# Five instead of three weight pieces converted beside the MoE, and the second layer from step 42

## The chip, the cores and the metric

The kernel runs on one NeuronCore of a Trainium2 chip. The metric is the device time of one execution in microseconds. A core has five engines that run side by side and wait for each other by semaphores: TensorE (PE in the profile; its weight loads are shown apart as PEld), VectorE (DVE), ScalarE (ACT), GpSimd (POOL) and SyncE (SP), which here only issues transfers. Each engine takes its instructions strictly in the order in which the program lists them.

## The reference

An attention of 4 batches, 8 heads, 576 tokens and 64 columns per head, with rotary embedding, feeds a gated MLP ("MoE" below):

```
scores = scale * matmul(rotate(q), rotate(k).T)
x      = softmax(scores) @ v              # back to (batch, 576, 512)
h      = maximum(x @ w_in, 0)             # w_in: 512 x 1024, first layer
gate   = sigmoid(conv3(h))                # three taps along the tokens
out    = (h * gate) @ w_out               # w_out: 1024 x 512, second layer
```

The weights come to the chip as 64-bit floats, seen as pairs of 32-bit integers. They are converted to fp32 on the chip.

## The kernel before

**Steps.** The attention is cut into 16 head pairs (p) of 5 row blocks (s), 80 steps in all. In a step PE forms one block of scores (L258), DVE takes the negated row maximum (`negm`, L266), ACT the exponential (`st`, L270), PE transposes the result one step later (`tp`, L318), ACT copies it out (`pt`, L197), and in the next five steps the product with v follows (L395), is copied to `xn` and normalised (`norm`, L413). POOL applies the rotary embedding to q and k (L188, L191; 18 instructions for a head pair), DVE transposes them into `qT` and `kT` (L231, L234).

**Two stages.** In steps 0 to 25 ("narrow") only attention and the conversion of weights run. From step 26 (`WIDE`) the MoE's work is woven in: `UNITS` says in which steps a first-layer unit (M1, L450 or L460) is formed, `HALVES` in which steps half a tile of the second layer (M2, L572: 48 matmuls into two PSUM tiles, then `oh` copied by ACT, L586, and added by DVE, L587). One step uses one pair of PSUM tiles `pm` (`m_pair`); whatever the step forms in `pm`, units, halves or products with v, shares that pair. The products with v of a head pair are formed in the steps that five divides (30, 35, 40, 45, 50).

**The order** is written out by hand: `at(n, rank, fn)` puts a piece of work into step n, and within a step the ranks sort it. All engines keep that order.

**The weights** are 16 pieces of 128x512: eight of `w_in` (0 to 7), then eight of `w_out` (8 to 15). A piece is one load of 512 KB, an ACT instruction (L598) and four DVE instructions: clamp (L601), shift (L607), low (L612), third (L617). A `w_out` piece is then split into a high part (ACT, L672) and a low part (POOL, four instructions, L669); of a `w_in` piece this is done later by `split_win` (L436, L439), in the steps of `SPLIT`. Pieces 0 to 12 are converted in steps 0 to 25, spread evenly by `COST`; `LATEW` lists the steps and ranks of the other three, between 25 and 35. M2 needs all eight `w_out` pieces, M1 the first four `w_in` low parts from step 46 and the other four from step 51.

**Memory.** The early pieces use the pool `ws`, whose memory goes to the MoE's tiles at step 26; the late pieces use a pool `wl` of their own, 12 KB of each partition, whose end at step 38 makes room for the tile `gb` (gated activations). `winh`, 16 KB of each partition, holds the high parts of `w_in`; nothing stands in it before step 39.

**The tail** after step 79 runs the rest of M1 and M2 alone.

Of the kernel before, what the change touches and what calls it, by code (L numbers as in the profile page):

```python
# [7 lines left out]
F32 = mybir.dt.float32  # L8
F32R = mybir.dt.float32r
# [11 lines left out]
def attention_moe_kernel(ctx, tc, q, k, v, w_in, conv_w, w_out, tab, tabx, out):  # L21
# [31 lines left out]

    winh = keep.tile([128, NK, DFF], F32R, name="winh")
    winp = ctx.enter_context(tc.tile_pool(name="winp", bufs=2 * NK + 1))
# [376 lines left out]
    def split_win(i):  # L432
        c, kk = divmod(i, NK)
        hi = winh[:, kk, 512 * c:512 * c + 512]
        lo = lows[kk, c] = winp.tile([128, 512], F32R, tag="w", name="wlo")
        nc.scalar.activation(out=hi, in_=raws[kk, c], func=AF.Copy)  # L436
        for o in range(0, 512, 128):
            w = slice(o, o + 128)
            nc.gpsimd.tensor_tensor(out=lo[:, w], in0=raws[kk, c][:, w], in1=hi[:, w].bitcast(F32), op=ALU.subtract)  # L439

    def emit_M1(blk, f, last=False):
# [6 lines left out]
        if plain(blk):  # L448
            for kk in range(NK):
                nc.tensor.matmul(  # L450
                    out=ps[:, 0:XW], lhsT=raws[kk, half][:, gs], rhs=xraw[kk, j], start=(kk == 0), stop=(kk == NK - 1)
                )
        else:
            n = 3 * NK
            i = 0
            for kk in range(NK):
                xs = xslot[b, kk, j]
                hi, lo = winh[:, kk, fs], lows[kk, half][:, gs]
# [132 lines left out]

    def to_f32(pool, bufs, w64, n):
        w32 = w64.bitcast(I32).rearrange("p (n t) -> p n t", t=2)
        h, l = w32[:, :, 1], w32[:, :, 0]
        t = pool.tile([128, n], I32, tag="wt", name="wt", bufs=bufs)[0:w64.shape[0]]

# [36 lines left out]
    def load_w(i):  # L633
        src, _, _, kk, c = WPIECES[i]
        pool, bufs = wpool(i)
        t = pool.tile([128, 512], I64, tag="w64", name="w64", bufs=bufs + 1)
        nc.sync.dma_start(out=t, in_=src[kk * 128:kk * 128 + 128, c:c + 512])
        stage[i] = t

    def conv_w_piece(i):  # L640
# [3 lines left out]
        def first():  # L644
            box["s"] = to_f32(*wpool(i), stage.pop(i), 512)
            box["s"][0]()
# [4 lines left out]
        def last():  # L651
            pool, bufs = wpool(i)
            if dl is None:
                box["w"] = raws[kk, c // 512] = winp.tile([128, 512], F32, tag="w", name="wr")
            else:
                box["w"] = pool.tile([128, 512], F32, tag="wf", name="wf", bufs=bufs)
            box["s"][4](box["w"])
            if i + 4 < WEARLY:
                load_w(i + 4)
            elif WEARLY <= i < len(WPIECES) - 2:  # L660
                load_w(i + 2)
            if dl is None:
# [39 lines left out]

    lctx = ExitStack()
    ws = wctx.enter_context(tc.tile_pool(name="ws", bufs=2))
    wl = lctx.enter_context(tc.tile_pool(name="wl", bufs=1, side="right"))

    def wpool(i):
        return (ws, 3) if i < WEARLY else (wl, 1)

    wcv = [conv_w_piece(i) for i in range(len(WPIECES))]  # L710
    WEARLY = len(wcv) - 3
    COST = (0, 0.5, 0.6, 0.85, 0.85)
    wsteps = [(0, wcv[0][0])]
    for i in range(WEARLY):
# [9 lines left out]
    LATEW = (  # L724
# [3 lines left out]
    )  # L728
    plan = {}
    onpe = (0, 0.2, 0.5, 1, 2, 2.4, 3, 4, 10)  # L730
    engines = {nc.tensor.engine, nc.vector.engine, nc.scalar.engine, nc.gpsimd.engine, nc.sync.engine}

    def at(n, rank, fn):
        plan.setdefault(n, []).append((rank, len(plan.get(n, [])), fn))

    def emit():
        with tc.manual_schedule(engines=engines):
# [83 lines left out]
            while any(plan.values()):  # L821
                n += 1
                late["n"] = n
                if n == WIDE:
# [87 lines left out]
```

## Time and profile before

| | |
|---|---|
| median of 3 runs | 475.98 us (475.81 to 476.61) |
| the profiled execution: its own time | 476.06 us |
| its span, first to last instruction | 474.3 us |
| PE busy / DVE busy / ACT busy / POOL busy | 457.1 / 352.3 / 327.9 / 293.0 us |
| granted TensorE clock | 1.00 throughout (the 2.4 GHz level) |

The engine shares are means over stages with different limits, so they are read stage by stage below. A step's start is taken as the start of its score matmuls (L258, eight instructions): step 36 begins at 152.0 us, 37 at 157.8, 40 at 172.7, 41 at 179.1, 42 at 184.9, 45 at 200.5 and 46 at 206.9 us.

### The profile page before, as it was taken

The numbers are of one execution on the slowest core, as the hardware profiler recorded it, in microseconds if no ns is written. First come the engines' busy times: TensorE is split into PE (matmuls) and PEld (weight loads), VectorE is DVE, ScalarE is ACT, GpSimd is POOL, SyncE is SP. The second block draws the span as 40 slices with busy tenths as digits, with TensorE's granted clock in tenths as the row PEclk, the third lists the DMA queues.
The fourth block names the chain that finished last, engine by engine and source line by source line (L and its number), as shares of the span: only waits on it lengthen the run. The fifth ranks groups of instructions, "written<-read, shape, count | busy, mean of one in ns | idle before, by whom it ended". The sixth has DMA issues, their size and how long they took to land.

```text
span 474.3 us, 12267 instructions
## 1 busy us (share of the span) xinstructions
PE 457.1 (96%) x4563; PEld 357.8 (75%) x4563; DVE 352.3 (74%) x641; ACT 327.9 (69%) x942; POOL 293.0 (62%) x478
## 2 busy tenths in 40 slices
PE   8789998989999999999999999999999999999997
PEld 7355655656666877778797978888797878899886
DVE  4799999986999886678677777866765747468921
ACT  2779889886897886879596877868686854244510
POOL 3859596998689694997939392938430332144610
PEclk9999999999999999999999999999999999999999
DMA  9798778362570716016161625135010000100011
GB/s 242 189 218 208 190 170 184 93 167 69 121 143 11 138 37 118 21 48 127 37 139 37 127 49 114 51 82 104 27 49 29 24 25 2 46 23 23 0 68 44
DMA packets 103183, 42.63 MB, mean 90 GB/s; under 512 B 94524, under 2 KB 97876, under 8 KB 103124
## 3 DMA queue, kind: packets, MB, share of 16 engines
q1 hardware_dynamic: 102672, 41.50, 37.3%
q8 instruction: 36, 0.59, 0.5%
q10 hardware_dynamic: 452, 0.35, 0.2%
q14 instruction: 23, 0.19, 0.1%
HBM read 37.04 MB, written 4.79 MB: 88 GB/s over the span
## 4 chain that ended last, share of the span: by engine, by line
PE 70%; DVE 13%; ACT 6%; POOL 3%; DMA 3%; issue 2%; SPq 1%; DVEq 0%; POOLq 0%; ACTq 0%
PE sp L258 11%; PE mt L552 11%; PE pm L395 10%; PE pm L572 10%; PE pm L460 9%; PE mt L460 7%; PE pm L450 5%; PE tp L318 5%; DVE negm L266 4%; ACT st L270 3%; POOL rk L188 2%; ACT pt L197 1%; DMA rq<-q 1%; DVE wt L601 1%; DVE wr L617 1%
## 5 line engine op out<-in xcount | busy, mean ns | idle before, releaser
L266 DVE TENSOR_REDUCE negm<-sp 128x1 f32<-128x576 f32 x144 | 102.5, 748 | 29.5 <-PE sp L258 22.2
L270 ACT ACTIVATE st<-sp,negm 128x576 f32<-128x576 f32 x128 | 93.8, 740 | 26.6 <-DVE negm L266 22.4
L258 PE MATMUL sp<-kT,qT 64*128 64x288 f32 (+4 forms) x556 | 94.5, 450 | 0.9 <-ACT kT L197 0.7
L197 ACT ACTIVATE pt<-tp 128x512 f32<-128x512 f32 (+3 forms) x176 | 84.5, 533 | 5.0 <-PE tp L318 4.3
L481 DVE SCALAR_TENSOR_TENSOR c<-rr,cw,c 128x288 f32<-128x288 f32 x128 | 79.3, 619 | 4.2
L499 POOL TENSOR_TENSOR gm<-c,gm 128x288 fp32r<-128x288 f32 (+4 forms) x72 | 45.7, 639 | 48.4 <-ACT gm L498 48.2
L188 POOL TENSOR_TENSOR rq<-rq,tabt 128x192 f32<-128x192 f32 x90 | 60.8, 709 | 18.1 <-DMA rq<-q 16.4
L188 POOL TENSOR_TENSOR rk<-rk,tabt 128x192 f32<-128x192 f32 x90 | 58.9, 687 | 8.0 <-DVE negm L266 4.3
L258 PEld LDWEIGHTS sp<-kT,qT 64*128 64x128 f32 (+1 forms) x556 | 44.8, 174 | 22.8 <-issue 9.8
L318 PEld LDWEIGHTS tp<-idf,st 64*128 64x128 f32 x1024 | 41.4, 139 | 21.9 <-ACT st L270 10.6
L318 PE MATMUL tp<-idf,st 64*128 64x64 f32 x1024 | 47.2, 227 | 6.5 <-ACT st L270 5.3
L395 PE MATMUL pm<-pt,vm 128*64 128x290 f32 x368 | 49.8, 411 | 0.4 <-ACT pt L197 0.4
L572 PE MATMUL pm<-wouth,gm 64*128 64x256 f32 x512 | 49.6, 284 | 0.0
L490 DVE SCALAR_TENSOR_TENSOR c<-c,rr 128x288 f32<-128x288 f32 x64 | 38.0, 614 | 9.5 <-ACT c L487 9.5
L479 DVE TENSOR_SCALAR c<-rr,cw 128x288 f32<-128x288 f32 x56 | 24.9, 444 | 23.2 <-ACT rr L471 22.9
L572 PEld LDWEIGHTS pm<-wouth,gm 64*128 64x128 f32 x512 | 41.5, 186 | 0.0
L420 POOL TENSOR_TENSOR xT<-xn,xT 128x290 fp32r<-128x290 f32 x18 | 16.0, 890 | 40.2 <-ACT xT L416 40.2
L395 PEld LDWEIGHTS pm<-pt,vm 128*64 128x64 f32 x368 | 25.5, 137 | 17.9 <-ACT pt L197 1.1
L460 PE MATMUL pm<-xT,winh 128*128 128x290 f32 x176 | 37.0, 302 | 0.0
L572 PE MATMUL pm<-woutl,gm 64*128 64x256 f32 x256 | 36.9, 278 | 0.0
L487 ACT ACTIVATE c<-c 128x288 f32<-128x288 f32 x64 | 28.5, 445 | 10.8 <-DVE c L481 10.8
L450 PE MATMUL pm<-xr,wr 128*128 128x290 f32 x128 | 34.5, 417 | 0.0
(127 smaller groups left out, 970.4 us busy)
## 6 DMA issues: line engine op xcount, KB each, us to landing
rq<-q SPq DMA_DIRECT2D x60, 144.0 KB
rk<-k SPq DMA_DIRECT2D x60, 144.0 KB
w<-moe_w_in SPq DMA_DIRECT2D x8, 512.0 KB
vm<-v SPq DMA_DIRECT2D x32, 128.0 KB
w<-moe_w_out SPq DMA_DIRECT2D x8, 512.0 KB
rb<-rd SPq DMA_DIRECT2D x16, 144.0 KB
out<-oh SPq DMA_DIRECT2D x18, 128.0 KB
rb<-rd SPq DMA_DIRECT2D x16, 128.0 KB
```

Of the source, the lines that this page charges most:

```text
L188: nc.gpsimd.tensor_tensor(out=y, in0=y, in1=tabt[:, a:a + 3], op=ALU.mult)
L197: nc.scalar.activation(out=out, in_=in_, func=AF.Copy, scale=1.0 if sc is None else sc)
L258: nc.tensor.matmul(out=out, lhsT=qt[64 * h:64 * h + 64, c], rhs=kt[64 * h:64 * h + 64, a:a + n], start=True, stop=True)
L266: reds.setdefault((p, s), []).append(lambda: nc.vector.tensor_reduce(out=nm, in_=sc, axis=AX.XY if len(sc.shape) == 3 else AX.X, op=ALU.ma ...
L270: lambda: nc.scalar.activation(out=dst, in_=sc, func=AF.Exp, bias=nm, scale=1.0, accum_out=sm)
L318: nc.tensor.transpose(ps[r][:, 64 * k:64 * k + 64], x[i], idf[i, i])
L395: nc.tensor.matmul(out=xp[64 * h:64 * h + 64, :], lhsT=vmain[p][:, h, i, :] if i < 4 else vrem[p % 2][:, h, :], rhs=pt[:, 2 * i + h if i < ...
L450: nc.tensor.matmul(out=ps[:, 0:XW], lhsT=raws[kk, half][:, gs], rhs=xraw[kk, j], start=(kk == 0), stop=(kk == NK - 1))
L460: nc.tensor.matmul(out=ps[:, 0:XW], lhsT=w, rhs=x_at(xs, e), start=(i == 0), stop=(i == n - 1))
L481: nc.vector.scalar_tensor_tensor(out=c, in0=r[:, j + e:j + e + HS], scalar=cw[:, 8 * e + f:8 * e + f + 1], in1=c, op0=ALU.mult, op1=ALU.add,)
L552: nc.tensor.matmul(out=ops[tt][:, 0:width], lhsT=g_tile(tt, f, e), rhs=w[:, f, cols], start=(f == 0 and i == 0), stop=(f == NF - 1 and i = ...
L572: nc.tensor.matmul(out=ps[r][:, 0:256], lhsT=g_tile(tt, f, e)[rows], rhs=w[rows, f, cols], start=(f == 0 and i == 0), stop=(f == NF - 1 an ...
```

## The change

`WEARLY` falls from 13 to 11: pieces 11 and 12 take the three late places of before, and pieces 14 and 15 get two new ones, in steps 35 to 38 and 38 to 41. The late pieces no longer have a pool of their own. A pool `highp` of two buffers of 8 KB takes the memory of `winh`: each late piece has one buffer for its load, its scratch and its result ("room"), and later the two buffers hold the high parts of the two halves of `w_in` (`wh`). The loads have steps of their own (`LOADW`). `gb` is there from step 26. M2 now starts at step 42: the halves of steps 37 and 39 move on, and two steps get a half that had none, 45 and 50. `SPLIT` moves by one or two steps.

```diff
-    winh = keep.tile([128, NK, DFF], F32R, name="winh")
+    highp = ctx.enter_context(tc.tile_pool(name="highp", bufs=2))
+    winh = {}
...
-        hi = winh[:, kk, 512 * c:512 * c + 512]
+        if c not in winh:
+            winh[c] = highp.tile([128, 4 * 512], F32R, tag="h", name="wh").rearrange("p (k n) -> p k n", k=NK)
+        hi = winh[c][:, kk, :]
...
-        t = pool.tile([128, 512], I64, tag="w64", name="w64", bufs=bufs + 1)
+        if i < WEARLY:
+            t = ws.tile([128, 512], I64, tag="w64", name="w64", bufs=4)
+        else:
+            room[i] = highp.tile([128, 4 * 512], F32, tag="h", name="room")
+            t = room[i].bitcast(I64)[:, 0:512]
...
-    WEARLY = len(wcv) - 3
+    WEARLY = len(wcv) - 5
...
-    HALVES = [37, 39, 42, 44, 47, 49, 52, 54, 57, 59, 62, 64, 67, 68, 72, 73, 76, 78]
+    HALVES = [42, 44, 45, 47, 49, 50, 52, 54, 57, 59, 62, 64, 67, 68, 72, 73, 76, 78]
...
-    SPLIT = (39, 40, 42, 43, 44, 45, 47, 48)
+    SPLIT = (40, 42, 44, 45, 46, 47, 49, 50)
...
+        ((35, 5.5), (36, 2.6), (36, 2.6), (37, 2.6), (37, 2.6)),
+        ((38, 5.5), (39, 2.6), (39, 2.6), (40, 2.6), (40, 2.6)),
     )
+    LOADW = (22, 23, 29, 33, 36)
```

The first place is DVE in steps 37 to 39, before. `c` rows are the MoE's convolution and gate, `xn` the normalising, `oh` the sum of a half of M2.

```order
L266 TENSOR_REDUCE negm<-sp 128x1 x2
L479 TENSOR_SCALAR c<-rr_1623,cw 128x288
L481 SCALAR_TENSOR_TENSOR c<-rr_1623,cw,c 128x288 x2
L413 TENSOR_TENSOR xn<-xn,rb 128x290 x2
L587 TENSOR_TENSOR oh<-oh,pm 128x256
L266 TENSOR_REDUCE negm<-sp 128x1 x2
L490 SCALAR_TENSOR_TENSOR c<-c,rr_1622 128x288
L490 SCALAR_TENSOR_TENSOR c<-c,rr_1623 128x288
L479 TENSOR_SCALAR c<-rr_1624,cw 128x288
L481 SCALAR_TENSOR_TENSOR c<-rr_1624,cw,c 128x288 x2
L266 TENSOR_REDUCE negm<-sp 128x1
```

The same place in the change. The `room` rows are the conversion of piece 14.

```order
L605 TENSOR_SCALAR room<-room 128x512
L611 TENSOR_SCALAR room<-room 128x512
L267 TENSOR_REDUCE negm<-sp 128x1 x2
L482 TENSOR_SCALAR c<-rr_1593,cw 128x288
L484 SCALAR_TENSOR_TENSOR c<-rr_1593,cw,c 128x288 x2
L414 TENSOR_TENSOR xn<-xn,rb 128x290
L616 SCALAR_TENSOR_TENSOR room<-room 128x512
L621 SCALAR_TENSOR_TENSOR room<-room 128x512
L414 TENSOR_TENSOR xn<-xn,rb 128x290
L267 TENSOR_REDUCE negm<-sp 128x1 x2
L493 SCALAR_TENSOR_TENSOR c<-c,rr_1592 128x288
```

Between the row maxima of steps 36 and 38 four conversion rows have come in and one `oh` row has gone; piece 15 follows in the same way in steps 39 and 40.

The second place is PE in step 37, before: scores, transposes, and the first of the 17 rows (48 matmuls) of a half of M2.

```order
L258 MATMUL sp<-kT,qT 128x288 x4
L318 MATMUL tp<-idf,st 128x64 x16
L355 MATMUL pm<-idf,st 128x64 x2
L572 MATMUL pm<-wouth,gm 128x256 x2
L572 MATMUL pm<-woutl,gm 128x256 x2
L572 MATMUL pm<-wouth,gm 128x256 x4
```

The same place in the change, steps 37 to 39; `pm<-xr` are the two units of M1 of step 38.

```order
L259 MATMUL sp<-kT,qT 128x288 x4
L319 MATMUL tp<-idf,st 128x64 x16
L356 MATMUL pm<-idf,st 128x64 x2
L259 MATMUL sp<-kT,qT 128x288 x4
L319 MATMUL tp<-idf,st 128x64 x16
L356 MATMUL pm<-idf,st 128x64 x2
L453 MATMUL pm<-xr,wr 128x290 x8
L259 MATMUL sp<-kT,qT 64x288 x4
```

Step 37 now holds scores and transposes alone, and step 39 (the `sp` of 64 rows) likewise; the 48 matmuls of each have moved on.

The third place is PE at the end of step 45, before: the products with v, straight behind the transposes (`tp`). The numbers tell the PSUM tiles apart.

```order
L318 MATMUL tp_3125<-idf_82,str_0_88 128x64
L395 MATMUL pm_3160<-pt_100,vm_2649 64x290 x8
L395 MATMUL pm_3160<-pt_100,vr_0_86 64x290 x2
L395 MATMUL pm_3161<-pt_100,vm_2649 64x290 x8
L395 MATMUL pm_3161<-pt_100,vr_0_86 64x290 x2
```

The same place in the change: the last two rows of the half that has come there, and the products behind it.

```order
L575 MATMUL pm_3011<-wouth_81,gm_1605 128x256
L575 MATMUL pm_3012<-wouth_81,gm_1605 128x256
L396 MATMUL pm_3011<-pt_102,vm_2517 64x290 x8
L396 MATMUL pm_3011<-pt_102,vr_0_88 64x290 x2
L396 MATMUL pm_3012<-pt_102,vm_2517 64x290 x8
L396 MATMUL pm_3012<-pt_102,vr_0_88 64x290 x2
```

The products write the two tiles that the half has just filled, so they wait until ACT and DVE have read them; before, no step held both. Step 50 is alike.

## Rows read from the trace of the kernel before

**Rows 1.** The page, part 1: busy time, share of the span, instructions of each engine.
```profile
PE 457.1 (96%) x4563; PEld 357.8 (75%) x4563; DVE 352.3 (74%) x641; ACT 327.9 (69%) x942; POOL 293.0 (62%) x478
```

**Rows 2.** Windows: stretch, length, busy PE PEld DVE ACT POOL, clock, DMA share, GB/s.
```profile
0.00:20.50 20.50, 16.20 (x119) 12.16 (x119) 11.61 (x29) 8.95 (x21) 12.64 (x25) 1.00 0.95 248
20.50:97.40 76.90, 70.42 (x814) 44.86 (x810) 74.59 (x130) 67.16 (x178) 58.76 (x91) 1.00 0.71 170
97.40:102.00 4.60, 3.67 (x34) 2.06 (x33) 4.23 (x13) 4.18 (x12) 4.60 (x8) 1.00 0.94 233
102.00:151.97 49.97, 48.67 (x410) 33.01 (x408) 43.73 (x67) 42.02 (x121) 42.58 (x65) 1.00 0.41 90
184.94:235.13 50.19, 49.53 (x582) 39.64 (x581) 35.89 (x63) 38.71 (x117) 41.76 (x74) 1.00 0.38 75
235.13:471.00 235.87, 235.70 (x2282) 200.91 (x2282) 156.02 (x298) 141.92 (x424) 104.51 (x173) 1.00 0.22 53
471.00:474.30 3.30, 0.00 (x0) 0.00 (x0) 0.42 (x1) 0.00 (x0) 0.00 (x0) 1.00 0.12 40
```

**Rows 3.** Windows, three stretches of the narrow stage.
```profile
26.60:43.40 16.80, 15.74 (x186) 10.19 (x186) 15.91 (x29) 14.08 (x39) 13.42 (x21) 1.00 0.90 209
43.40:60.10 16.70, 16.09 (x200) 10.59 (x200) 16.38 (x30) 15.18 (x42) 10.90 (x17) 1.00 0.78 199
50.00:60.00 10.00, 9.84 (x121) 6.57 (x119) 9.92 (x18) 8.91 (x25) 5.80 (x10) 1.00 0.68 170
```

**Rows 4.** Groups by line, DVE, 20.5 to 97.4 us: count, busy, mean ns.
```profile
L612 DVE SCALAR_TENSOR_TENSOR wt<-w,wt 128x512 int32<-128x512 int32 x12 | 9.9, 825 | 0.3
L601 DVE TENSOR_SCALAR wt<-wt 128x512 f32<-128x512 f32 x12 | 7.0, 581 | 0.0
L617 DVE SCALAR_TENSOR_TENSOR wr<-w,wt 128x512 int32<-128x512 int32 x8 | 6.7, 832 | 0.1
L607 DVE TENSOR_SCALAR wt<-wt 128x512 int32<-128x512 int32 x12 | 6.6, 553 | 0.3
```

**Rows 5.** Timeline of DVE, the last late piece: start, length, operation.
```profile
140.71 0.81 DVE L601 TENSOR_SCALAR wt<-wt 128x512 f32<-128x512 f32 x1
141.55 0.69 DVE L607 TENSOR_SCALAR wt<-wt 128x512 int32<-128x512 int32 x1
145.79 1.08 DVE L612 SCALAR_TENSOR_TENSOR wt<-w,wt 128x512 int32<-128x512 int32 x1
146.97 1.10 DVE L617 SCALAR_TENSOR_TENSOR wf<-w,wt 128x512 int32<-128x512 int32 x1
```

**Rows 6.** Chain of waits: the M2 halves of steps 37 and 39.
```profile
159.60 2.90 PE pm L572 x47
...
169.96 2.91 PE pm L572 x48
```

**Rows 7.** Windows, from the row maxima of step 36 on.
```profile
153.25:169.30 16.05, 16.05 (x162) 12.48 (x159) 13.67 (x24) 12.57 (x37) 12.48 (x19) 1.00 0.53 102
153.25:173.87 20.62, 20.62 (x240) 16.80 (x238) 17.25 (x29) 16.04 (x47) 17.05 (x26) 1.00 0.41 80
153.25:178.84 25.59, 25.59 (x282) 19.70 (x278) 22.14 (x38) 19.71 (x57) 22.02 (x35) 1.00 0.40 81
```

**Rows 8.** Timelines of PE, ACT and DVE: the end of the half of step 44.
```profile
200.34 0.28 PE L572 MATMUL pm<-wouth,gm 64*128 64x256 f32 x2
...
200.66 0.38 ACT L586 ACTIVATE oh<-pm 128x256 f32<-128x256 f32 x1 [0.69 <-PE pm L572]
...
201.07 0.42 DVE L587 TENSOR_TENSOR oh<-oh,pm 128x256 f32<-128x256 f32 x1 [1.41 <-ACT oh L586]
```

**Rows 9.** Timeline of DVE: the transpose of k in step 45, with its wait.
```profile
207.22 0.78 DVE L234 STREAM_TRANSPOSE kT<-rk 128x576 f32<-128x576 f32 x1 [2.01 <-POOL rk L191]
```

**Rows 10.** Timelines of ACT and PE where the MoE begins, with their waits.
```profile
110.33 0.53 ACT L475 ACTIVATE c<-rr,cw 128x288 f32<-128x288 f32 x1 [3.44 <-POOL woutl L669]
...
111.33 0.39 PE L355 MATMUL pm<-idf,st 64*128 64x64 f32 x2 [0.79 <-ACT pt L197]
```

More of the change, by code (lines that the diff above doesn't have):

```diff
@@ L457, in emit_M1 @@
                 xs = xslot[b, kk, j]
-                hi, lo = winh[:, kk, fs], lows[kk, half][:, gs]
+                hi, lo = winh[half][:, kk, gs], lows[kk, half][:, gs]
                 for w, e in ((hi, 0), (hi, 1), (lo, 0)):
@@ L590, in m2_half, with to_f32 @@
         return first, second
-    def to_f32(pool, bufs, w64, n):
+    def to_f32(pool, bufs, w64, n, t=None):
         w32 = w64.bitcast(I32).rearrange("p (n t) -> p n t", t=2)
         h, l = w32[:, :, 1], w32[:, :, 0]
-        t = pool.tile([128, n], I32, tag="wt", name="wt", bufs=bufs)[0:w64.shape[0]]
+        if t is None:
+            t = pool.tile([128, n], I32, tag="wt", name="wt", bufs=bufs)[0:w64.shape[0]]
         def first():
@@ L634, in load_w @@
         src, _, _, kk, c = WPIECES[i]
-        pool, bufs = wpool(i)
-        t = pool.tile([128, 512], I64, tag="w64", name="w64", bufs=bufs + 1)
+        if i < WEARLY:
[3 more added lines that the diff above has]
+            t = room[i].bitcast(I64)[:, 0:512]
         nc.sync.dma_start(out=t, in_=src[kk * 128:kk * 128 + 128, c:c + 512])
@@ L644, in first @@
         def first():
-            box["s"] = to_f32(*wpool(i), stage.pop(i), 512)
+            box["s"] = to_f32(ws, 3, stage.pop(i), 512, room[i].bitcast(I32)[:, 1024:1536] if i in room else None)
             box["s"][0]()
@@ L651, in last @@
         def last():
-            pool, bufs = wpool(i)
             if dl is None:
                 box["w"] = raws[kk, c // 512] = winp.tile([128, 512], F32, tag="w", name="wr")
+            elif i < WEARLY:
+                box["w"] = ws.tile([128, 512], F32, tag="wf", name="wf", bufs=3)
             else:
-                box["w"] = pool.tile([128, 512], F32, tag="wf", name="wf", bufs=bufs)
+                box["w"] = room[i][:, 1536:2048]
             box["s"][4](box["w"])
@@ L659, in last @@
                 load_w(i + 4)
-            elif WEARLY <= i < len(WPIECES) - 2:
-                load_w(i + 2)
             if dl is None:
@@ L701, in m2_units @@
         return [lambda t=t, i=i: emit_M2(t, i) for t in range(a, b) for i in range(4)]
-    lctx = ExitStack()
     ws = wctx.enter_context(tc.tile_pool(name="ws", bufs=2))
-    wl = lctx.enter_context(tc.tile_pool(name="wl", bufs=1, side="right"))
-    def wpool(i):
-        return (ws, 3) if i < WEARLY else (wl, 1)
+    room = {}
     wcv = [conv_w_piece(i) for i in range(len(WPIECES))]
-    WEARLY = len(wcv) - 3
+    WEARLY = len(wcv) - 5
     COST = (0, 0.5, 0.6, 0.85, 0.85)
@@ L804, in emit @@
             for i, when in enumerate(LATEW):
-                if i < 2:
-                    at(22 + i, 19, lambda i=i: load_w(WEARLY + i))
+                at(LOADW[i], 19, lambda i=i: load_w(WEARLY + i))
                 for (n, rank), u in zip(when, wcv[WEARLY + i]):
@@ L832, in emit @@
                     gpool = ctx.enter_context(tc.tile_pool(name="gpool", bufs=1))
-                    late["g"] = [gpool.tile([128, 2, NF, RA], F32R, name="gm")]
+                    late["g"] = [gpool.tile([128, 2, NF, n], F32R, name=nm) for nm, n in (("gm", RA), ("gb", RING - RA))]
                     for t in late["rr"]:
                         nc.vector.memset(t[:, 0:XW + 1:XW], 0.0)
-                if n == WIDE + 12:
-                    lctx.close()
-                    late["g"].append(ctx.enter_context(tc.tile_pool(name="gb", bufs=1)).tile([128, 2, NF, RING - RA], F32R, name="gb"))
                 while plan.get(n):
```

## The prediction

> **What bounds the kernel now.** I read the page's first part, then the windows by stage, then the timelines of the stages that the change touches. The page says that PE is busy for 457.1 of 474.3 us [rows 1]. The change leaves every matmul as it is, so the time moves only as far as PE's idle time does, and the idle time is a budget of 17.2 us. The windows show where it lies [rows 2]: 20.50 - 16.20 = 4.3 us up to 20.5 us; 76.90 - 70.42 = 6.5 in the narrow stage; 0.9 + 1.3 = 2.2 from 97.4 to 152; 0.7 from 184.9 to 235.1; 0.2 from there to the last matmul; 3.3 behind it. From 153.25 to 178.84 PE shows none at all [rows 7].
>
> In the narrow stage the limit is DVE, with 74.59 of 76.90 us (97%), but PE is close behind with 92% [rows 2]. From step 36 on it is PE alone, and DVE has slack: from 153.25 to 178.84 it is busy for 22.14 of 25.59 us [rows 7].
>
> **Step 1: two pieces leave the narrow stage.** Its four DVE instructions make a piece cost 0.58 + 0.55 + 0.83 + 0.83 = 2.79 us there [rows 4], so DVE loses 5.6 us, and ACT and POOL some work too. DVE falls to about 69.0 us, below PE's 70.42. What is late next is PE, whose floor no edit here lowers. So the gain is what PE's idle time can give up, at most 6.5 us, and not 5.6 us for certain. The nearest rows give the bounds. Where PE and DVE together run best for ten us, PE is busy for 98.4%; over the five steps 43.4 to 60.1 us for 16.09 of 16.70 (96.3%); over the five before, 15.74 of 16.80 (93.7%) [rows 3]. 70.42 us of PE at these rates take 71.6, 73.1 and 75.2 us: a gain of 5.3, 3.8 or 1.7 us. I take 3.8, because DVE would still be at about 95%, and two engines that wait for each other in every step won't both reach 98% throughout.
>
> Here a rule of the Trainium skill speaks against me. Perfetto Trace Analysis (Identifying the Most-Contended Engine) says that matmul busy time doesn't show how near TensorE is to its limit, and that the busy share of the weight loads does. In the narrow stage that share is 44.86 of 76.90 us, 58%, against 85% after 235 us. By that rule PE has room, and the 5.6 us would come back whole (first rival below). The trace agrees only in part: in the best ten us PE's busy row reaches 98% with weight loads at 66% [rows 3], so a gapless PE at that mix of matmuls shows no more.
>
> **Step 2: the passage into the MoE.** ACT's first tap waits 3.44 us for POOL's low part of the last early piece, and PE then waits 0.79 us [rows 10]. POOL has two low parts fewer ahead of it, but the piece in question stands in the same place behind the rotary work. I take 0.4 us off, between 0 and 0.8.
>
> **Step 3: the halves of steps 37 and 39 go.** A half takes PE 2.90 and 2.91 us [rows 6]; PE loses 5.8 us of work in a stretch where it had no idle time. If nothing else held the stretch, it would end 5.8 us earlier and the move would be free.
>
> **Step 4: two pieces come in between, in steps 36 to 40.** A late piece costs DVE 0.81 + 0.69 + 1.08 + 1.10 = 3.68 us [rows 5], more than an early one. Two `oh` additions of 0.42 us [rows 8] leave. I follow DVE from 153.25 us without a pause. Up to the row maximum of step 39 (169.30 before) it was busy for 13.67 us [rows 7]; less 0.42, plus piece 14, makes 16.93, so it comes at 170.2, 0.9 us later than before although PE's step is shorter. Up to the maximum of step 40 it was 17.25 us; less 0.84, plus 3.68, plus the first two instructions of piece 15 (1.50), makes 21.59: 174.8 against 173.87. Up to the end of step 40 it is 22.14 - 0.84 + 7.36 = 28.7, so DVE ends at 181.9, not 178.8. PE needs the maximum and the exponential of each step for its next transposes. With the maximum of step 39 at 170.2, transposes and products of step 40 start some 1.8 us earlier than before, and step 42 with them; every pause of DVE on the way comes off that. So DVE becomes the limit of steps 36 to 40, and of the 5.8 us that PE gave up, the stretch returns 1.0 (from 1.8 down to -0.5, a stretch half a us longer). The other 4.8 us are new idle time of PE.
>
> ACT's four new instructions lie in the same steps, where ACT was busy for 19.71 of 25.59 us [rows 7], and two `oh` copies leave: no cost. POOL gets two low parts and keeps one split fewer; it had 25.59 - 22.02 = 3.6 us free there [rows 7]. On SP the loads of the last three pieces wait for the low part two pieces before; behind them stand loads of v and of the reciprocal sums that are needed a step or more later. No cost either; if that cover is gone, DVE waits, and the third rival has the price.
>
> **Step 5: the halves come back in PE's own time.** From step 42 on PE has 0.7 us of idle time in 50 [rows 2], so the 5.8 us are paid in full: +5.8.
>
> **Step 6: a new wait in steps 45 and 50.** The products with v now need the tiles that the half has just filled. Behind a half, ACT's copy ends 0.42 us after PE's last matmul (200.62 to 201.04) and DVE's addition 0.45 us later [rows 8]. PE's first product needs ACT's copy alone, the second, ten matmuls later, DVE's addition. Queued behind it on PE are the products, and the next scores. No step before holds this wait; I take 0.45 us each, 0.9 in all, from 0 (the second tile covers the first) to 2.0 in all (DVE's addition stands behind the transpose of k, which waited 2.0 us for POOL in step 45 [rows 9]). Against it, POOL has one split fewer ahead of that k; PE's 0.7 us of idle time there may shrink by 0.3 (0 to 0.7).
>
> **The sum.** -3.8 - 0.4 - 1.0 + 5.8 + 0.9 - 0.3 = +1.2 us on the execution's own 476.06 us: 477.3. The median of the runs, 475.98, lies 0.1 lower: I predict 477.2 us. All ends together: -5.3 - 0.8 - 1.8 + 5.8 + 0 - 0.7 = -2.8, and -1.7 + 0 + 0.5 + 5.8 + 2 + 0 = +6.6.
>
> **The rivals.** About 0.2% (1 us) is what a measurement of this kernel can tell from no change.
>
> First, faster: in the narrow stage DVE's time counts in full, since DVE leads the chain there at 97% and every row maximum stands behind conversion rows. Then -5.6 - 0.8 - 1.8 + 5.8 + 0.5 - 0.3 = -2.2: 473.8 us. The rule named under step 1, of the Trainium skill, would give this one. Against it stands PE's 92%. It decides as soon as PE's idle time from 20.5 to 97.4 us falls below about 1.5 us. Chance 0.15.
>
> Second, about even: PE reaches there what it shows in its best ten us, and the gain is 5.0; -5.0 - 0.4 - 1.0 + 5.8 + 0.9 - 0.3 = 0: 476.0 us. Chance 0.22.
>
> Third, slower still: POOL. M1 of step 46 needs two splits that now stand behind the rotated k of step 45, and POOL is 2.0 us late with that k already [rows 9]. The half in step 45 puts M1 off by 2.9 us [rows 6]. If DVE's delay of 3.1 us at the end of step 40 reaches POOL in full, PE waits 2.0 + 3.1 - 2.9 = 2.2 us there: 479.4 us. Against it stand the 3.6 us that POOL had free. Chance 0.15.
>
> The forecast has 0.48; its own range is 476.4 to 478.7. The range over all cases, 474.4 to 479.8, leaves about 0.1 on each side. Slower by over 0.2%: 0.15 + most of 0.48, 0.56; within: most of the even case and the low end of the forecast, 0.25; faster: 0.15 and the edge of the even case, 0.19.
>
> **What the profile after would show.** The narrow stage ends 3 to 5 us earlier, with PE at 96% or more and DVE at about 95%. Between steps 36 and 41 PE has some 5 us of idle time, put down to ACT's exponentials and behind them DVE, with DVE near 100%; step 42 starts some 5 us earlier than before. From there on PE is solid but for a gap of about half a us in steps 45 and 50, named ACT `oh`. Wrong would be: PE without gaps in steps 37 to 40 (then DVE had room); an unmoved narrow stage (then PE, or the loads, held it); gaps of a us or more at steps 46 and 51 (POOL).

## The result, and the profile after

The changed kernel takes 480.1 us (median of 6 runs, 479.1 to 480.6) against 476.3 us (475.8 to 476.6) of the kernel before beside it: ratio 1.0078, 95% interval 1.0064 to 1.0092, 3.8 us slower. Forecast were 477.2 us, with a range of 474.4 to 479.8. The direction was right; the loss is three times the forecast one and lies 0.3 us above the range. (The late pieces of the changed kernel are 11 to 15: 11 to 13 stand in the three late places of before, 14 and 15 in the new ones.)

The profiled execution took 479.14 us (span 477.4), the fastest of the six, so its trace explains +3.1 us; the rest is the spread, 1.5 us here against 0.8 before. The page of the changed kernel, part 1, answers to [rows 1]:

```profile
PE 459.4 (96%) x4563; PEld 359.2 (75%) x4563; DVE 351.5 (74%) x641; ACT 328.3 (69%) x942; POOL 294.9 (62%) x478
```

The same instructions as before, every count unchanged; what differs is when they run and, by a us or two, how long. The windows of the changed kernel, stage by stage (columns as in [rows 2]; the fourth is steps 36 to 41, the fifth 42 to 44, the sixth 45 to 50):

```profile
20.50:93.90 73.40, 69.39 (x814) 44.62 (x810) 69.59 (x122) 64.86 (x174) 56.03 (x86) 1.00 0.73 164
93.90:98.58 4.68, 3.70 (x34) 2.09 (x34) 4.08 (x12) 4.35 (x14) 4.23 (x7) 1.00 0.99 240
98.58:147.46 48.88, 48.57 (x408) 33.15 (x408) 42.28 (x67) 42.38 (x121) 40.58 (x60) 1.00 0.46 102
147.46:179.99 32.53, 29.03 (x237) 20.10 (x237) 28.78 (x50) 23.25 (x69) 30.21 (x48) 1.00 0.34 72
179.99:196.69 16.70, 16.17 (x190) 13.28 (x192) 12.35 (x22) 13.94 (x41) 13.11 (x23) 1.00 0.53 98
196.69:236.54 39.85, 38.82 (x464) 31.42 (x460) 25.96 (x48) 27.13 (x79) 33.01 (x63) 1.00 0.32 70
236.54:474.10 237.56, 237.38 (x2310) 202.09 (x2308) 156.27 (x293) 143.26 (x429) 104.96 (x173) 1.00 0.22 53
```

The narrow stage is 3.5 us shorter, with PE and DVE both at 95%. The fourth line is the surprise: PE has 3.5 us of idle time in 32.5, but neither DVE (28.8 us busy) nor POOL (30.2) fills the stretch. (Busy time understates the room: run without a gap, the same matmuls need 27.95 us, as a run below shows.) The same two stretches of the kernel before:

```profile
151.97:184.94 32.97, 32.97 (x334) 25.12 (x333) 25.80 (x47) 24.98 (x72) 28.13 (x48) 1.00 0.35 75
184.94:200.46 15.52, 15.21 (x192) 12.72 (x193) 10.82 (x20) 12.49 (x37) 10.00 (x16) 1.00 0.48 80
```

There PE was solid. With 96 matmuls (5.8 us) less, steps 36 to 41 became 0.44 us shorter, and steps 42 to 44, whose matmuls are unchanged, 1.18 us longer. Step by step, after against before: up to step 36, -4.51 us; steps 36 to 41, -0.44; 42 to 44, +1.18; step 45, +3.52 (9.92 for 6.40); 46 to 49, -0.06; step 50, +3.51; the rest, -0.1. Sum +3.1. The first of these varies from profile to profile: in 13 profiles of kernels with five late pieces, which are the same program up to there, step 36 starts at 147.46 to 149.62 us (median 148.57), in the three with the pieces of before at 151.97 to 153.10 (median 152.97). The medians lie 4.4 us apart.

Where PE waits in steps 38 and 40, by its timeline in the changed kernel:

```profile
156.53 1.71 PE L259 MATMUL sp<-kT,qT 64*128 64x288 f32 x7 [1.43 <-ACT st L271]
...
164.81 0.70 PE L259 MATMUL sp<-kT,qT 64*128 64x288 f32 x2
166.77 0.99 PE L259 MATMUL sp<-kT,qT 64*128 64x288 f32 x5 [1.26 <-ACT str L271]
```

The scores themselves wait, for the exponential that empties their PSUM tile. Both waits stand one step behind those that lost their halves.

### The profile page after: what moved, and what is told of

Read it like the earlier page. It is cut to its first block, busy times and chain, and to the rows that moved or that the text cites. A ratio compares the mean times of both kernels' runs of the same rounds, so it can differ in the third digit from the quotient of the medians.

```text
span 477.4 us, 12263 instructions
## 1 busy us (share of the span) xinstructions
PE 459.4 (96%) x4563; PEld 359.2 (75%) x4563; DVE 351.5 (74%) x641; ACT 328.3 (69%) x942; POOL 294.9 (62%) x478
## 4 chain that ended last, share of the span: by engine, by line
PE 73%; POOL 7%; DVE 7%; ACT 7%; DMA 3%; issue 2%; SPq 1%; POOLq 0%; DVEq 0%; ACTq 0%
PE sp L259 12%; PE mt L555 11%; PE pm L575 10%; PE pm L463 10%; PE pm L396 9%; PE mt L463 7%; PE tp L319 6%; PE sp L396 3%; PE pm L453 3%; ACT st L271 3%; DMA rq<-q 2%; DVE negm L267 2%; ACT pt L198 2%; POOL rq L189 2%; POOL rk L189 2%
## 5 line engine op out<-in xcount | busy, mean ns | idle before, releaser
L259 PE MATMUL sp<-kT,qT 64*128 64x288 f32 (+4 forms) x556 | 96.9, 450 | 4.2 <-ACT st L271 2.2
L259 PEld LDWEIGHTS sp<-kT,qT 64*128 64x128 f32 (+1 forms) x556 | 45.8, 174 | 27.3 <-issue 8.4
L189 POOL TENSOR_TENSOR rk<-rk,tabt 128x192 f32<-128x192 f32 x90 | 57.6, 673 | 6.2 <-DMA rk<-k 4.4
L575 PEld LDWEIGHTS pm<-wouth,gm 64*128 64x128 f32 x512 | 42.5, 185 | 0.0
L396 PEld LDWEIGHTS pm<-pt,vm 128*64 128x64 f32 x368 | 25.5, 136 | 18.8 <-ACT oh L589 1.1
L575 PE MATMUL pm<-woutl,gm 64*128 64x256 f32 x256 | 38.2, 278 | 0.0
L463 PE MATMUL pm<-xT,wh 128*128 128x290 f32 x176 | 37.0, 302 | 0.0
```

The costliest lines, as they stand in the source:

```text
L189: nc.gpsimd.tensor_tensor(out=y, in0=y, in1=tabt[:, a:a + 3], op=ALU.mult)
L259: nc.tensor.matmul(out=out, lhsT=qt[64 * h:64 * h + 64, c], rhs=kt[64 * h:64 * h + 64, a:a + n], start=True, stop=True)
L396: nc.tensor.matmul(out=xp[64 * h:64 * h + 64, :], lhsT=vmain[p][:, h, i, :] if i < 4 else vrem[p % 2][:, h, :], rhs=pt[:, 2 * i + h if i < ...
L575: nc.tensor.matmul(out=ps[r][:, 0:256], lhsT=g_tile(tt, f, e)[rows], rhs=w[rows, f, cols], start=(f == 0 and i == 0), stop=(f == NF - 1 an ...
```

## The experiments

All are compared with the kernel before on the same chip; "us against before" is (ratio - 1) x 476.5. Lengths of stretches come from the starts of the score matmuls in each profile. They can be compared where PE's granted clock is the same: in five of the profiles below it stands at 0.50 (the 1.2 GHz level) for 3.4 us in step 38 or 40, and the matmuls there take longer. These are named where they are used; in all others it is 1.00 in steps 36 to 45.

| run | ratio (95%) | us | 36 to 41 | 42 to 44 | 45 |
|---|---|---|---|---|---|
| before | 1 | 0 | 32.97 | 15.52 | 6.40 |
| changed | 1.0078 (1.0064-1.0092) | +3.7 | 32.53 | 16.70 | 9.92 |
| changed, again | 1.0070 (1.0049-1.0092) | +3.3 | 32.30 | 16.71 | 9.92 |
| pieces without DVE rows | 1.0031 (1.0017-1.0046) | +1.5 | 30.93 | 15.52 | 9.90 |
| before, halves moved | 1.0152 (1.0126-1.0179) | +7.2 | 30.73 | 15.52 | 10.65 |
| that, units spread | 1.0086 (1.0069-1.0103) | +4.1 | 27.95 | 16.73 | 10.64 |
| no pieces, old halves | 0.9914 (0.9891-0.9936) | -4.1 | 32.96 | 15.52 | 6.41 |
| products elsewhere | 1.0047 (1.0030-1.0064) | +2.2 | 32.30 | 16.70 | 9.49 |
| units spread (clock 0.50 in step 40) | 1.0062 (1.0039-1.0086) | +3.0 | 32.79 | 15.76 | 9.90 |
| units spread, products elsewhere | 1.0024 (1.0013-1.0035) | +1.1 | 31.57 | 16.84 | 9.46 |

**Is it DVE's conversion?** The changed kernel without the eight DVE rows:

```diff
 def part(k):
-    return lambda: box["s"][k]()
+    return lambda: i < len(WPIECES) - 2 and box["s"][k]()
...
```

> The changed kernel, but the four VectorE instructions each of pieces 14 and 15 are left out (the values of these two pieces of the second layer's weights are wrong by that; their load, ScalarE instruction, high and low parts stay, so the matmuls are the same). Theory DVE: VectorE holds steps 36 to 41 of the changed kernel, so 7.4 us less of it there lets PE get through them with few gaps; of the 5.8 us of halves that went, at least 3 more come back: about 476.5 us, and the row maximum of step 41 has nothing to wait for. Rival POOL: GpSimd, busy for 32.1 of 34.4 us from 148.0 to 182.4, holds the stretch through the transpose of k that waits 2.55 us for it; then VectorE's time is no matter, and the kernel stays within 1 us of the changed one: 479.1 to 480.1 us, with a longer wait at that transpose.

Measured 478.7 us, 2.2 us less than the changed kernel by the ratios. Steps 42 to 44 are back at 15.52, but steps 36 to 41 give up only 1.6 us more than in the changed kernel. Neither theory held: without the eight rows (6.1 us in the changed kernel's profile) 3.8 of the 5.8 us still don't return.

**The halves alone.** In the kernel before:

```diff
-    HALVES = [37, 39, 42, 44, 47, 49, 52, ...
+    HALVES = [42, 44, 45, 47, 49, 50, 52, ...
```

> The kernel before with nothing but the list of M2 halves of the changed kernel (42, 44, 45, 47, 49, 50 for 37, 39, 42, 44, 47, 49). Theory: without the two late pieces the steps 37 and 39 become 5.8 us shorter in full; what stays are the waits behind the halves of steps 45 and 50, 0.6 us each, so 476.3 + 1.2 = 477.5 us. Rival: the chain of row maximum, exponential and transposes, or POOL, holds steps 37 to 41 also without the pieces; then 2 us or more of the 5.8 do not come back: 479.5 us or more.

Measured 483.9 us, +7.2, more than the whole change costs. The rival held: with no piece in these steps, 2.24 of 5.81 us come back. The timelines of PE, DVE and ACT in this run, steps 37 and 38, show why:

```profile
158.94 1.24 PE L258 MATMUL sp<-kT,qT 64*128 64x288 f32 x8
160.21 1.42 DVE L266 TENSOR_REDUCE negm<-sp 128x1 f32<-128x576 f32 x2 [0.57 <-PE sp L258]
161.00 0.74 ACT L270 ACTIVATE st<-sp,negm 128x576 f32<-128x576 f32 x1 [0.65 <-DVE negm L266]
161.73 0.73 ACT L270 ACTIVATE st<-sp,negm 128x576 f32<-128x576 f32 x1
161.89 1.72 PE L258 MATMUL sp<-kT,qT 64*128 64x288 f32 x7 [1.15 <-ACT st L270]
163.21 0.22 PE L318 MATMUL tp<-idf,st 64*128 64x64 f32 x1
```

From the first score matmul of step 37 to the first transpose of its result go 4.3 us, through one engine after the other, each with idle time ahead of it: no engine is full, the round trip is the limit. PE has 1.7 us of scores and transposes in such a step. The halves of steps 37 and 39 were what it did meanwhile. Step 37, from its first score to the first one of step 38, takes 2.95 us here (158.94 to 161.89) and took 4.53 before: 1.58 of the half's 2.90 us come back.

In step 45 of this run the wait is worse than in the changed kernel, 10.65 - 6.40 - 2.9 = 1.35 us (and 11.33 - 6.41 - 2.9 = 2.0 in step 50). Its DVE timeline there:

```profile
206.14 0.78 DVE L234 STREAM_TRANSPOSE kT<-rk 128x576 f32<-128x576 f32 x1 [2.01 <-POOL rk L191]
206.84 0.20 DVE L240 STREAM_TRANSPOSE kT<-rk 128x64 f32<-128x64 f32 x1
206.97 0.38 DVE L587 TENSOR_TENSOR oh<-oh,pm 128x256 f32<-128x256 f32 x1
```

The addition that frees the second tile stands behind the transpose of k, which waits for POOL.

**Cover put back.** The same kernel, the first-layer units of steps 36 and 38 spread:

```diff
-    UNITS.update({n: 2 for n in (36, 38, 41, ...
+    UNITS.update({n: 1 for n in (36, 37, 38, 39)})
+    UNITS.update({n: 2 for n in (41, ...
```

> The kernel before with the list of halves of the changed kernel, as in the run with the halves alone (483.9 us), and with the two first-layer units each of steps 36 and 38 spread over 36, 37, 38 and 39, one each. Theory: in steps 37 and 39 PE has only 1.7 us of scores and transposes of its own, while the way from the scores over row maximum and exponentials to the next transposes takes about 4 us, and 3.6 of the 5.8 us stay as waits for the exponentials; with one unit of 2.1 us in each of the four steps most of that is covered: 483.9 - 2 to 3.5 = 480.4 to 481.9 us. Rival (ACT's or DVE's work in these steps sets their length, whatever the order): 483.9 us.

Measured 481.3 us, 3.1 us less by the ratios, 2.6 by the medians and 1.7 between the two profiled executions. The windows of steps 36 to 41, halves moved (first) and with the units spread (second):

```profile
153.10:183.83 30.73, 29.03 (x238) 20.10 (x237) 25.12 (x45) 24.02 (x70) 26.98 (x46) 1.00 0.35 66
```

```profile
152.97:180.92 27.95, 27.95 (x238) 19.43 (x237) 23.48 (x42) 21.58 (x64) 24.51 (x41) 1.00 0.38 65
```

The same matmuls, and PE is solid: 5.02 of the 5.81 us return, where 2.24 did. That shows the round trip as the cause of most of what the moved halves cost in steps 36 to 41. Not all of the 2.8 us lasts: steps 42 to 44 take 16.73 us in place of 15.52, so step 45 starts 1.6 us earlier, counted from step 36.

**The same with the pieces.** The spread units in the changed kernel, alone and with the other PSUM tiles of the paragraph on steps 45 and 50 below:

> The changed kernel with the units of steps 36 and 38 spread over 36 to 39, one each. Theory: the 3.6 us that the missing cover costs shrink as without the pieces, but the pieces' eight VectorE rows stay and VectorE was busy for 29.5 of 34.4 us there, so 1.5 to 3 us come back: 477.1 to 478.6 us. Rival (VectorE or POOL sets the length): 480.1 us.

> The changed kernel with both repairs: units spread over steps 36 to 39, and the products with v of steps 45 and 50 in the PSUM tiles of the transposes. Theory: the repairs add up, 0.9 us below the run with the spread units alone: 476.2 to 477.7 us, about the kernel before. Rival: with the first wait gone the second is late elsewhere, no better than either alone.

Measured 479.8 and 478.4 us. The spread returns little here; in the second run steps 36 to 41 take 31.57 us (32.79 in the first), against 27.95 without pieces:

```profile
148.58:180.15 31.57, 28.75 (x237) 20.04 (x237) 29.80 (x50) 22.68 (x67) 29.43 (x47) 1.00 0.34 74
```

Up to step 45 the two are the same program. What makes the first one longer is PE's clock, which fell in step 40:

```profile
169.89:173.30 3.41, 3.41 (x15) 1.70 (x16) 3.34 (x6) 2.04 (x7) 3.41 (x6) 0.50 0.00 0
```

At the full clock DVE (29.80, 94%) and POOL (29.43, 93%) are now the busiest engines; which of them sets the length is not shown. So steps 36 to 41 have two floors that lie close: the round trip (30.7 us) and the pieces' work (31.6). Removing either alone meets the other; that is why the first run above told so little.

**The gain alone.** Pieces 14 and 15 left out, halves and splits in their old steps:

```diff
+    for f in (6, 7):
+        for t in (wouth, woutl):
+            nc.scalar.activation(out=t[:, f, :], in_=raw[0]["q"]..., func=AF.Copy)
...
-    for i, when in enumerate(LATEW):
+    for i, when in enumerate(LATEW[0:3]):
```

> The changed kernel without pieces 14 and 15 (never loaded or converted; their rows of the second layer's weights hold values of q, put there before the narrow stage), and with the M2 halves and the splits in the steps of the kernel before. So the narrow stage stays relieved, and steps 37 and 39 keep their halves. Theory (the halves were the cover of the softmax's round trip): all the loss comes from moving the halves and from the two pieces between; here only the gain is left, 4.4 us at step 36: 476.3 - 4.4 = 471.9 us. Rival (the relief of the narrow stage does not last, later stages give it back whatever stands there): 474 us or more.

Measured 472.9 us, -4.1 (interval -5.2 to -3.0): the relief of the narrow stage is real and lasts to the end. Its windows up to step 36 and from there to 42:

```profile
99.46:149.00 49.54, 48.48 (x410) 32.99 (x408) 43.41 (x67) 41.90 (x121) 41.03 (x62) 1.00 0.44 95
149.00:181.96 32.96, 32.96 (x333) 25.11 (x332) 25.71 (x47) 24.98 (x72) 28.11 (x48) 1.00 0.35 76
```

With the halves in place, steps 36 to 41 are those of the kernel before, to 0.01 us. All of the loss, 7.8 us between this run and the changed kernel, comes from moving the halves (with the splits) and from the two pieces.

**The wait behind the halves of steps 45 and 50.** The products get other PSUM tiles:

```diff
-    xp = m_tile()[:, 0:n] if "m" in psum else spare(n)
+    if late["n"] in (45, 50):
+        xp = t_tile()[:, 0:n]
+    else: ...
```

> The changed kernel, but the products with v of steps 45 and 50 go into the PSUM tiles of the transposes instead of the pair that the half has just filled. Theory: steps 45 and 50 grew by 3.5 us each, 2.9 for the half and 0.6 for the wait behind it; without the wait they grow by 2.9, and the kernel takes 480.1 - 1.2 = 478.9 us. Rival: the wait only moves on, to the transposes of steps 46 and 51, which now wait for the copies of the products: 480.1 us, no change.

Measured 479.0 us, 1.5 us less by the ratios (the intervals overlap). PE at the end of the half of step 45, in the changed kernel and then in this run:

```profile
200.82 0.39 PE L575 MATMUL pm<-wouth,gm 64*128 64x256 f32 x2
201.58 2.17 PE L396 MATMUL pm<-pt,vm 128*64 128x290 f32 x16 [0.36 <-ACT oh L589]
```

```profile
201.97 0.40 PE L578 MATMUL pm<-wouth,gm 64*128 64x256 f32 x2
202.29 1.93 PE L399 MATMUL tp<-pt,vm 128*64 128x290 f32 x14
```

From the last half matmul to the first product 0.76 us, then 0.32; the step shrinks from 9.92 to 9.49, step 50 likewise, and nothing grows behind. The wait is worth 0.9 us in the two steps.

**The 1.2 us of steps 42 to 44.** DVE and then POOL in step 40 of the changed kernel:

```profile
174.84 0.78 DVE L235 STREAM_TRANSPOSE kT<-rk 128x576 f32<-128x576 f32 x1 [2.55 <-POOL rk L192]
175.54 0.20 DVE L241 STREAM_TRANSPOSE kT<-rk 128x64 f32<-128x64 f32 x1
175.67 1.21 DVE L616 SCALAR_TENSOR_TENSOR room<-room 128x512 int32<-128x512 int32 x1
176.91 0.69 DVE L621 SCALAR_TENSOR_TENSOR room<-room 128x512 int32<-128x512 int32 x1
...
178.36 1.38 DVE L267 TENSOR_REDUCE negm<-sp 128x1 f32<-128x576 f32 x2
```

```profile
165.33 2.19 POOL L675 TENSOR_TENSOR woutl<-room,wouth 128x128 fp32r<-128x128 f32 x4
167.48 1.93 POOL L421 TENSOR_TENSOR xT<-xn,xT 128x290 fp32r<-128x290 f32 x2
169.37 3.78 POOL L189 TENSOR_TENSOR rk<-rk,tabt 128x192 f32<-128x192 f32 x6
```

The transpose of k waits for POOL, whose rotary work stands behind piece 14's low part; conversion and the row maximum of step 41 are queued behind it. The low part is not all that makes POOL late. Its rotary work on q, ahead of all this, had waited for the load of q (first row); before, POOL came to it later, behind an `xT` that waited 3.57 us for ACT, and found it there (other two rows):

```profile
158.66 4.54 POOL L189 TENSOR_TENSOR rq<-rq,tabt 128x192 f32<-128x192 f32 x6 [2.32 <-DMA rq<-q]
```

```profile
163.34 0.80 POOL L420 TENSOR_TENSOR xT<-xn,xT 128x290 fp32r<-128x290 f32 x1 [3.57 <-ACT xT L416]
164.10 3.85 POOL L188 TENSOR_TENSOR rq<-rq,tabt 128x192 f32<-128x192 f32 x6
```

All 17 profiles in which a half has left steps 37 to 39 have this wait for q, 1.68 to 3.44 us; the two with the halves in their old steps have none. Counted from step 36, POOL begins with k at 18.5 us in the kernel before with halves moved and units spread, and at 18.8 before: the steps got shorter, POOL's work on k did not come sooner. No run moves the load, so what it costs stays open.

Two runs moved POOL's work (the low part behind the rotary work; then the split of step 40 two steps later as well), and one moved the transpose behind the row maximum:

```diff
-    at(late["n"] + 1, 0.12, lambda: (high(), low()))
+    at(late["n"] + 1, 0.12, high)
+    at(late["n"] + 1, 18.5 if i == 14 else 0.12, low)
...
-    SPLIT = (40, 42, 44, 45, ...
+    SPLIT = (42, 43, 44, 45, ...
```

```diff
-    at(n - 5 + i * (n - 15 < WIDE) if early ...   # emit_TQ
+    at(n - 5 + i * (n - 20 < WIDE) if early ...
```

> The changed kernel, but the low part of piece 14 (GpSimd, 2.19 us) stands behind the rotary work of k in step 38, not ahead of it. Theory: VectorE's transpose of k in step 40 waits 2.55 us for that rotary work, which puts off the row maximum of step 41 and costs steps 42 and 43 some 1.2 us; with 2.19 us less ahead of it the wait is 0.4 us: 478.9 us. Rival: VectorE is the limit there anyway, and the wait is only time in which it would have run into another one: 480.1 us, no change.

> The changed kernel with the low part of piece 14 behind the rotary work of k, as before (480.2 us, no gain: the split of the first layer's weights in step 40 then waited for that low part, because it writes the same memory, and held up ACT), and that split now two steps later. Theory: the 1.2 us lost in steps 42 and 43 come from the transpose of k that waits for POOL; with neither wait left they come back: 478.9 us. Rival: VectorE's own work in steps 39 to 41 is what makes the row maximum of step 41 late, and whatever wait goes, another takes its place: 480.1 us.

> The changed kernel, but VectorE's transpose of the k that step 45 needs stands behind the row maximum of step 41, not in step 40 ahead of it. Theory: the 1.2 us of steps 42 and 43 come from that transpose, which waits for POOL with the conversion and the row maximum queued behind it; with nothing behind it the row maximum of step 41 is on time, steps 42 to 44 take 15.5 us as in the kernel before and not 16.7, and nothing else moves: 478.9 us, ratio to before 1.005. Rival (VectorE's own work makes that row maximum late): steps 42 to 44 stay at 16.7 us, ratio 1.008.

Ratios 1.0068 (1.0042-1.0094), 1.0089 (1.0068-1.0109), 1.0078 (1.0055-1.0101): no gain in any. Yet steps 42 to 44 take 15.53, 15.53 and 15.52 us in the three, as before the change. What was won went elsewhere: in the second run into step 45 (10.65 us), in the other two into steps 36 to 41 (35.66 and 33.68 us).

That the transpose in DVE's queue is the cause of the 1.2 us fits, but these profiles don't show it. In all three the clock fell in steps 38 or 40, as here in the one with the moved transpose, where PE had waited 2.18 us for an exponential until 159.18:

```profile
160.52:163.93 3.41, 3.41 (x25) 2.76 (x22) 3.38 (x5) 1.45 (x6) 3.41 (x5) 0.50 1.11 277
```

Step 38 takes 8.12 us there and in the second run, for 6.55 in the changed kernel; in the first run step 40 takes 10.73 for 8.47. And a slower PE can shorten steps 42 to 44 by itself: the run with units spread leaves the transpose where it is, its clock fell in step 40, and they take 15.76 us; its twin at the full clock takes 16.84. Nor is the wait at the transpose enough: without DVE's rows it is as long (2.54 us), and steps 42 to 44 take 15.52. So the gain of these edits and the lower clock can't be told apart here, and the cause of the 1.2 us stays open.

The record has a hint of the gain alone: of the 26 runs of these edits, the repeat below included, four have a mean clock of 0.999 or more, and they lie 1.6 to 2.5 us above the kernel before on their chips; the six such runs among the changed kernel's twelve lie 2.7 to 4.4 above. That is about the 1.2 us expected, but picked after the fact, and none of the four was profiled.

The last pair ran the changed kernel and the moved transpose beside each other:

> The changed kernel once more, beside the next one, to see how its stretch from step 36 to 42 varies. Theory: the four VectorE rows of piece 14 take either 2.6 us in all (with the POOL rows beside them slower) or 4.0 us, which is the 1.3 us between the changed kernel's own runs (479.2 and 480.5 us); 480.1 us median, ratio 1.008. Rival: the runs differ in the narrow stage, by the loads, and piece 14 takes 2.6 us each time.

> The changed kernel with the transpose of k behind the row maximum of step 41, once more. Theory: in its first profile steps 42 to 44 gave 1.2 us back and piece 14 ran at its slow speed (4.0 us, 1.2 us later at step 42), so the two cancelled by chance; compared run for run with the changed kernel on the same chip it is 0.5 to 1.2 us faster: ratio to before 1.006. Rival: the later transpose itself brings the slow speed, by moving POOL against VectorE; then both are even, 1.008.

Ratios 1.0070 and 1.0076 (1.0051-1.0100): even. Again 15.52 us in steps 42 to 44, again steps 36 to 41 longer, 33.53 against 32.30, and again the clock at 0.50 for 3.4 us in step 38 (8.12 us for 6.55). In both profiles of that edit, and in that of the low part moved alone, piece 14 ran at a slower speed (last section; step 37 takes 3.98 us for 3.23), which the edits come too late to order; whether they have to do with it stays open. The first theory of the pair fell: piece 14 took 2.9 us in the second profile of the changed kernel (480.26 us), which lost its time ahead of step 36 (148.78 for 147.46).

**Towards a faster kernel.** Spread units and products elsewhere, plus the first taps of the units of steps 36 to 43 on ACT (1.0040, 1.0025-1.0055); plus, on top of that, the low part and the split moved (1.0018, 1.0006-1.0029); or, in place of the taps, the transpose moved (1.0024, 1.0007-1.0041):

> The run with units spread and the products in other PSUM tiles (478.4 us, 1.0024 of before), and the first tap of the eight units of steps 36 to 43 on ScalarE, not VectorE (some 0.65 us each). Theory: with the cover back, VectorE holds steps 36 to 41 (29.8 of 31.6 us), so 3 to 5 us less of it there gives back 2 us or more: ratio to before 0.998 or less, about 475.5 to 476.5 us. Rival: POOL's rotary work (29.4 of 31.6 us) holds them as well: 1.002.

> The run above with the low part of piece 14 behind the rotary work of k and the split of step 40 two steps later. Theory: VectorE's transpose of k no longer waits for POOL, which gives up to 1 us more in steps 41 to 43: ratio 0.996. Rival: with VectorE relieved it has the time to wait there, no difference to the run above.

> The run with units spread and the products in other PSUM tiles (ratio to before 1.0024), with the transpose of k moved as in the run above. Theory: steps 42 to 44 took 16.8 us there for the same reason, so 1.2 us come back: ratio 1.000. Rival: 1.0024, VectorE has no time to spare with the cover back.

Four late pieces, halves from step 39, taps on ACT (1.0003, 0.9992-1.0014), or taps on DVE and the transpose moved (1.0020, 1.0007-1.0033):

> Four late pieces instead of five: piece 15 in the place of piece 14, halves from step 39 (one has to go to step 45), units of step 36 spread over 36 and 37, taps of the second block on ScalarE, products of step 45 in the PSUM tiles of the transposes. Theory: half of the narrow stage's gain (2.1 us), one half moved (2.9 us) of which some 2.4 come back in step 37 with its unit as cover, 0.2 us of wait in step 45, 0.5 us for VectorE: -2.1 + 2.9 - 2.4 + 0.2 + 0.5 = -0.9 us against before, ratio 0.998. Rival: the narrow stage pays nothing for one piece alone (ACT or PE holds it): ratio 1.002.

> Four late pieces (piece 15 in the place of 14), halves from step 39 with one in step 45, units of step 36 spread over 36 and 37, products of step 45 in the PSUM tiles of the transposes, all taps on VectorE as in the kernel before, and the transpose of k moved as in the first run of these. Theory: the run with four pieces and taps on ScalarE was even with before (1.0003), and its steps 42 to 44 took 17.0 us in place of 15.5; without the wait at the transpose and without VectorE's waits for the taps 1 to 1.5 us come back: ratio 0.997 to 0.998, about 475.3 us. Rival (VectorE is full again with the taps): 1.000 or more.

None beats the kernel before, and no theory's ratio came; the two rivals of the moved transpose (1.0024; 1.000 or more) did. Taking the first taps off DVE (26.46 us busy in steps 36 to 41, not 29.80) shortens these steps by 0.7 us alone, so DVE's time is not their only limit. In all five, steps 36 to 41 take 30.6 to 31.3 us and steps 42 to 44 take 16.7 us or more, with the transpose moved too: so with the cover back something else makes them late. The pieces are not needed for it: the kernel before with halves moved and units spread has none in these steps, its POOL waits 3.44 us for the load of q, its transpose of k 2.55 us for POOL, and steps 42 to 44 take 16.73 us. That POOL keeps up less, the faster steps 36 to 41 go by, fits, but no run isolates it.

## Why the prediction was wrong

**Step 1** held: 3.5 us in the narrow stage against 3.8, and 4.1 us to the end with the later steps left as before. The 5.6 us that the first rival took whole did not come: PE's busy row stands at 94.5% with weight loads at 61%, and DVE beside it at 94.8%. The rule on weight loads of the Trainium skill (Perfetto Trace Analysis, Identifying the Most-Contended Engine) had pointed to that rival; the trace doesn't agree with the 5.6 us, but which engine kept the rest is not shown. **Step 2** forecast 0.4 us; the profile has 1.0 up to step 36. That was partly luck: ACT's first tap waits 2.16 us for POOL and not 3.44, and PE's wait behind it is gone, but in the changed kernel's second profile both are as before (3.45 and 0.82).

**Step 4** is where the sum failed, on a premise of step 3. It had steps 36 to 41 return 1.0 of the 5.8 us, as DVE's busy time would allow, and step 42 and all behind it follow at PE's own pace. The profile has 0.44 returned and 1.18 lost again in steps 42 to 44, together 1.7 of the 1.9 us by which it missed the sum. The premise is step 3's "If nothing else held the stretch, it would end 5.8 us earlier and the move would be free", with DVE's busy time as the only thing that could hold it. The halves alone, with no piece in the way, return 2.24 us. I read "it is PE alone, and DVE has slack" off [rows 7], and never asked what PE would wait for with less to do. Row maximum, exponential and transposes stand in series behind the scores in every step of the trace; I never added them up.

So 0.44 for 1.0 is nearly the right number for half the reason. The round trip is a second floor that lies 0.8 us below that of the pieces' work, and no engine's busy time shows it; the sign "DVE near 100%" did not come (28.78 of 32.53 us, 88%). The 1.18 us of steps 42 to 44 were put at nothing. In the profile the row maximum of step 41 stands behind a transpose that waits for POOL, and [rows 9] has that wait five steps later; but that this wait is the cause is not shown, as said above.

**Step 5** held: 2.9 us a half. **Step 6** named the right wait: 0.62 and 0.61 us (9.92 - 6.40 - 2.9, 9.92 - 6.41 - 2.9) against 0.45; with the tiles changed 0.9 us of it went. What its upper bound stood for, DVE's addition behind a transpose that waits for POOL, is real (3.4 us for both steps in the run with the halves alone, above the bound of 2.0), but not in the changed kernel. POOL's relief (-0.3) did not show: -0.06 in steps 46 to 49.

By terms, forecast to profile: step 36, -4.2 to -4.5; steps 36 to 41, -1.0 to -0.4; 42 to 44, 0 to +1.2; the halves with their waits, +6.7 to +7.0; POOL, -0.3 to -0.1. That is +1.2 to +3.1 (the terms are rounded), and the spread of the runs adds the rest. The first two rivals took the gain of the narrow stage too large (5.6 and 5.0 us for 3.5); the third one's place (step 46) shows nothing: 5.16 us in both. POOL does come late with a k, but with that of step 40, five steps earlier.

## What to carry to other kernels

Work that a busy engine does between two ends of a dependency chain is also its cover: before moving it, time the chain without it (here 4.3 us from the scores to their transposes, with 1.7 us of PE's own work in a step), not only the busy time of the others. Where two floors lie close, removing one cause shows little; test each with the other gone. In queues in strict order, look at what is queued behind each wait in the stretch that gets faster, not only at the wait. Before step lengths of two profiles are compared, compare the granted clock in those steps.

## What the hardware showed beside

The same DVE rows of piece 14 have two speeds. In the changed kernel:

```profile
153.67 0.67 DVE L605 TENSOR_SCALAR room<-room 128x512 f32<-128x512 f32 x1
154.37 0.57 DVE L611 TENSOR_SCALAR room<-room 128x512 int32<-128x512 int32 x1
...
157.94 0.68 DVE L616 SCALAR_TENSOR_TENSOR room<-room 128x512 int32<-128x512 int32 x1
158.66 0.69 DVE L621 SCALAR_TENSOR_TENSOR room<-room 128x512 int32<-128x512 int32 x1
```

In the second run with the moved transpose:

```profile
154.59 1.02 DVE L605 TENSOR_SCALAR room<-room 128x512 f32<-128x512 f32 x1
155.65 0.90 DVE L611 TENSOR_SCALAR room<-room 128x512 int32<-128x512 int32 x1
...
159.95 1.08 DVE L616 SCALAR_TENSOR_TENSOR room<-room 128x512 int32<-128x512 int32 x1
161.06 0.97 DVE L621 SCALAR_TENSOR_TENSOR room<-room 128x512 int32<-128x512 int32 x1
```

2.61 against 3.97 us. The first pair goes by what POOL does beside it. In the fast case the pair begins while POOL's low part runs, which takes 2.38 us; in the slow case the low part (1.98 us, from 152.38) has ended, and the two `gm` subtractions run beside the pair, 1.95 us (1.72 in the fast case, where they begin as the pair ends). So it is in all seven profiles with this order: low part 2.37 or 2.38 us and a fast pair in four, 1.98 us and a slow pair in three. Beside the second pair POOL's rotary work ran in the slow case; in the fast case POOL waited for the load of q until 158.66. The fast case's last row begins together with that work: DVE keeps its 0.69 us there, and POOL's first two instructions take 1.91 us (1.60 in the slow case). The Trainium skill, GPSIMD Engine Reference (Specifications), says that GpSimd shares its memory interfaces with VectorE and contends with VectorE instructions that have two inputs in SBUF or run in a two-port mode. That one of the two engines is slower wherever these rows meet agrees, with the numbers above; in which mode the rows run, the trace doesn't show. What puts POOL early or late against the first pair, no run here shows.
